# A planned order replaced by a written list, and key products in half-width tiles, in the first part of a delta-rule attention and two MoE layers

## The chip, the cores and the metric

One core of one Trainium2 chip runs the whole program in one launch. The metric is the device time in microseconds. The five engines are TensorE (PE; its weight loads are shown apart as PEld), VectorE (DVE), ScalarE (ACT), GpSimd (POOL) and SyncE (SP), which issues most of the DMA transfers.

## The reference

Three stages run one after the other. The first is a delta-rule attention over 4 batches, 8 heads, 768 steps and a head width of 48, which is written as a recurrence:

```python
k_n = k / (norm(k, axis=-1) + 1e-06)
for t in range(S):
    y[:, :, t] = einsum('bhd,bhde->bhe', q[:, :, t], state)
    v_old = einsum('bhde,bhd->bhe', state, k_n[:, :, t])
    state = state + beta[:, :, t] * einsum('bhd,bhe->bhde', k_n[:, :, t], v[:, :, t] - v_old)
```

Its output, as 3072 tokens of 384 numbers, goes through a dense layer `g = h * clip(h + 3, 0, 6) / 6` with `h = x @ w_in` (384 to 2048) and `g @ w_out`. The last stage sends every token to the one of 8 experts with the largest gate logit, `max(x @ w1, 0) @ w2` with a hidden width of 1024, and scales the result by the gate's probability.

## The kernel before

**The first part** (up to line 1156) computes the attention in chunks of 64 steps. One iteration `it` is one chunk of one pair of batches: 12 chunks by 2 pairs make 24 iterations, and four iterations make a group `g`, of which there are 6. In one iteration ScalarE and VectorE (in the first group; GpSimd later) split the normalised keys into two float16 halves `Kbd`, a transposing DMA turns them into `KG` or `KTb`, and TensorE forms the products of the keys with each other, `pG` (`g_stream`, line 603). Per head `u` these are two 64x64 blocks, one for each batch of the pair, on 64x64 tiles of the array, each in three products of halves. The blocks' two 32x32 diagonal blocks lie in columns 0 to 31 for the first 32 rows and in columns 32 to 63 for the others, so ScalarE copies them to `Dt` in four copies of 32 partitions each (lines 624 to 627). The columns 0 to 31, which hold the off-diagonal block, go to `MC`.

When a group's four iterations are copied, `t_stream` (line 634) transposes `Dt` on VectorE into `Bt`, multiplies it by beta on GpSimd (line 645) and clears `Xp` on ScalarE. Then `s_stream` (the solver, line 651) does 31 steps of two VectorE instructions each (`sub`, `Xp`), every step on what the step before has left. `z_stream` transposes the result, splits it into `TT` and multiplies it with `MC` (`pZ`). The two `chain` streams carry the state from chunk to chunk (`pR`, `pW`, `pS`), `o_stream` and `x_stream` make the attention's output `pO` and transpose it (`pX`, `xTH`, `xTL`), and `m_stream` (line 1029) runs the first 7 of the 16 hidden tiles of the dense layer for each chunk of 256 tokens: nine matmuls `ph`, four steps on ScalarE, VectorE, ScalarE and GpSimd (`t`, `t`, `gH`, `gL`), and six matmuls `py`. `wi_stream` and `wo_stream` prepare the weights of these tiles (`nws` on VectorE).

**The order** is not written by hand. Every stream is a generator that yields one instruction, or one burst of matmuls, at a time. `drive` (line 1078) asks a planner, `Clock`, when each stream's next instruction could start by its cost formulas, takes those that could start at about the same time on one engine, and emits the one with the smallest due number (`DUE`). `pin` ties each instruction to the one before on its engine, so that the queues of all engines and of SP run in the emitted order. In the planner's formulas a VectorE instruction that reads two SBUF operands waits for a running GpSimd instruction (`shared`, `unshared`), and not the other way round. `take` gives a stream one of three PSUM banks.

**The rest** is not touched by the change: the other 9 hidden tiles in six blocks of 512 tokens (line 1438 on, with the routing), and the experts (line 1548 on).

Of the kernel before, what the change touches and what calls it, by code (L numbers as in the profile page):

```python
# [24 lines left out]
class Op:  # L25

    tiles = 2
# [11 lines left out]
class Clock:  # L39


    def __init__(self, tc):
        self.tc, self.last = tc, {}
        self.free = dict(pe=0.0, act=0.0, dve=600.0, pool=3100.0, dma=0.0)
        self.columns = {}
        self.written, self.read, self.bus, self.issue = {}, {}, 0.0, 0.0
        self.slot, self.count, self.parts = {}, {}, {}
        self.runs, self.phase, self.tick, self.warm = [], 0.0, 0, False
        self.mode = 128, False
        self.place, self.end = {}, dict(act=0.0, dve=0.0)  # L50

    def tile(self, pool, shape, dt, tag, bufs, name):
        t = pool.tile(shape, dt, tag=tag, name=name, bufs=bufs)
        n = self.count[tag] = self.count.get(tag, -1) + 1
        self.slot[t.name] = (tag, n % bufs)
        return t

    def keys(self, ap):

        n = ap.name  # L60
        if n in self.parts:
            return [(n, x) for x in self.parts[n](ap)]
        return [self.slot.get(n, n)]

    def cost(self, op):

        n = 1
        for d in (op.ins[0] if "reduce" in op.fn.__name__ else op.out).shape[1:]:
            n *= d
        if "dma" in op.fn.__name__:  # L70
            return 40
        half = (op.ins[-1] if op.eng == "pe" else op.out).dtype in (FP16, FP32R, BF16)
        if op.eng == "pe":
            if op.ins[-1].dtype == FP32R:
                return n / 2.2
            if op.ins[-1].shape[0] <= 64:
                return max(32 if op.ins[-1].shape[0] == 64 else 25.2, n / 2.4) / op.tiles
            return max(25.5, n / 2.4 + 2.5) if half else 0.85 * max(n, 128)
        fn = op.fn.__name__
        pointers = sum(x.free_size() == 1 for x in op.ins[1:])  # L80
        if op.eng == "act":
            return (52 if op.ins[0].space == PSUM else 109) + 95 * (pointers > 0) + 84 * (len(op.outs) > 1) + 0.836 * n
        if op.eng == "dve":
            if half and fn == "tensor_copy":
                return 64 + 0.26 * n
            if fn == "memset":
                return 60 + (0.38 if half else 0.82) * n
            if fn == "transpose":
                return 70 + 1.06 * n
            if fn == "reciprocal":  # L90
                return 70 + 6 * n
            if fn == "tensor_scalar" and op.ins[0].space != PSUM:
                return 66 + 0.52 * n + 60 * (pointers > 0)
            return 70 + (0.52 if all(x.dtype == FP16 for x in op.ins) else 1.04) * n + 60 * (pointers > 0)
        if op.eng == "pool":
            if fn in ("memset", "tensor_copy"):
                return 80 + 0.81 * n
            wide = op.out.dtype == FP32R or op.out.shape[-1] == 32
            return 60 + (2.5 if wide else 2.15) * n
        raise ValueError(op.eng)  # L100

    def places(self, op):

        r, w = {}, (op.out.space, op.out.start_partition())
        for x in op.ins:
            r.setdefault(x.space, x.start_partition())
        return r, w

    def held(self, op):

        r, w = self.places(op)
        now = self.place.setdefault(op.eng, ({}, {}))
        return any(now[0].get(m, x) != x for m, x in r.items()) or now[1].get(w[0], w[1]) != w[1]

    def shared(self, op):

        if op.eng != "dve" or op.fn.__name__ in ("memset", "transpose", "tensor_reduce", "reciprocal"):
            return False
        wide = [x for x in op.ins if x.free_size() > 1]
        sb = [x for x in wide if x.space != PSUM]  # L120
        if op.fn.__name__ in ("tensor_copy", "tensor_scalar"):
            return bool(sb) and op.out.space != PSUM
        return len(sb) > 1

    def unshared(self, t):

        for a, b in reversed(self.runs):
            if b < t:
                break
            if a <= t:  # L130
                return b
        return t

    def matmul(self, op, t):

        n, tick = op.out.free_size(), int((t + self.phase) * 3 / 10240)
        rows = op.ins[-1].shape[0]
        half = op.ins[-1].dtype in (FP16, FP32R, BF16)
        while self.tick < tick:
            self.warm = self.columns.get(self.tick, 0.0) >= (3060 if self.warm else 3350)  # L140
            self.tick += 1
        self.columns[tick] = self.columns.get(tick, 0.0) + n * (1 if half else 2) * rows / 128
        mode, last = (32 if rows <= 32 else 64 if rows <= 64 else 128, op.ins[-1].dtype == FP32R), self.mode
        self.mode = mode
        turn = 90 * (mode[0] != last[0]) + (0 if mode[1] == last[1] else 85 if mode[1] else 13)
        if self.warm:
            return turn + self.cost(op)
        if rows <= 64:
            return turn + max(53.4 if rows == 64 else 42, n / 1.2) / op.tiles
        return turn + (max(27, n / 1.2) if half else 1.7 * max(n, 128))  # L150

    def ready(self, tiles):
        return max([self.free["pe"]] + [self.written.get(k, 0.0) for x in tiles for k in self.keys(x)])

    def start(self, ops):
        t = 0.0
        for op in ops:
            t = max([t] + [self.read.get(k, 0.0) for x in op.outs for k in self.keys(x)] + [self.written.get(k, 0.0) for x in op.ins for k in self.keys(x)])
        t = max(self.free[ops[0].eng], t + {"pe": 54, "pool": 77}.get(ops[0].eng, 33))
        if ops[0].eng in self.end and "dma" not in ops[0].fn.__name__ and self.held(ops[0]):  # L160
            t = max(t, self.end[ops[0].eng] + 13)
        return self.unshared(t) if self.shared(ops[0]) else t

    def pin(self, op):
# [5 lines left out]
        self.last[op.eng] = ins  # L170

    def emit(self, ops):
        t = t0 = self.start(ops)
        for op in ops:
            t += self.cost(op) if op.eng != "pe" else self.matmul(op, t)
            self.pin(op)
        self.free[ops[0].eng] = t
        if "dma" in ops[0].fn.__name__:
            o = ops[0].out
            n = 2 if o.dtype == FP16 else 4  # L180
            turn = "transpose" in ops[0].fn.__name__
            rate = 200 if turn else 170 if n * o.shape[-1] < 512 else 320
            for d in o.shape:
                n *= d
# [1445 lines left out]
```

## Time and profile before

| | us |
|---|---|
| median of three runs (lowest, highest) | 999.49 (997.93, 1002.62) |
| the profiled execution | 1003.64 |
| its span, first to last instruction | 1001.9 |
| first part, up to the first matmul of line 1459 | 507.6 |

| engine | busy us in the span | share |
|---|---|---|
| PE | 885.3 | 88% |
| DVE | 586.2 | 59% |
| ACT | 569.0 | 57% |
| POOL | 433.2 | 43% |

A share is a mean over stages with different limits, so it says little by itself. The first part has to be read in stretches, and the sections below do that. A row of the trace names the engine, the line (L36 is the helper that emits every instruction of the first part), the operation, and the tiles, output first.

### The profile page before, as it was taken

To read this page: it belongs to the slowest core of one execution; us is meant where nothing else is said; L and a number is where in the kernel's file an instruction comes from. 1 tells how busy PE (TensorE), PEld (TensorE's weight loads), DVE (VectorE), ACT (ScalarE), POOL (GpSimd) and SP (SyncE) were. 2 spreads that over 40 slices of the span, in tenths; PEclk is the share of its full clock that TensorE was granted. 3 is DMA by queue.
4 is the path that set the end of the run, shared out by engine and by line. 5 is a ranking of instruction groups with operands and counts; after the bars stand their busy time and mean duration, and the time that the engine had idled before them with its cause. 6 is when DMAs were issued, how large, how long until landed. Compare 5 with 4: busy or idle time off the path is not lost.

```text
span 1001.9 us, 27659 instructions
## 1 busy us (share of the span) xinstructions
PE 885.3 (88%) x11454; PEld 819.2 (82%) x11454; DVE 586.2 (59%) x1611; ACT 569.0 (57%) x1195; POOL 433.2 (43%) x446
## 2 busy tenths in 40 slices
PE   1423898889988899999989999999999999999997
PEld 1412888889888798888878899898899999999996
DVE  7888997888979789653487545554534211222221
ACT  4757889779888876755557333323334542455521
POOL 5255565455546524423343204223104936755761
PEclk9999799999999989999999999999999999999999
DMA  7978797996998956566365432332116734434500
GB/s 127 190 145 158 126 179 135 176 139 124 211 198 110 200 112 123 125 155 208 118 218 172 131 93 97 128 96 97 53 61 240 228 105 153 147 114 141 172 21 20
DMA packets 255080, 138.89 MB, mean 139 GB/s; under 512 B 199587, under 2 KB 239845, under 8 KB 254944
## 3 DMA queue, kind: packets, MB, share of 16 engines
q1 hardware_dynamic: 247120, 118.82, 53.5%
q0 software_dynamic: 7280, 17.41, 5.2%
q8 instruction: 91, 1.49, 0.6%
q10 hardware_dynamic: 544, 0.80, 0.2%
q14 instruction: 45, 0.37, 0.1%
HBM read 71.56 MB, written 35.50 MB: 107 GB/s over the span
## 4 chain that ended last, share of the span: by engine, by line
PE 61%; DVE 14%; ACT 8%; issue 7%; DMA 6%; POOL 4%; SPq 0%; POOLq 0%; ACTq 0%
PE ph L1459 11%; PE ph L1250 9%; PE py L36 5%; PE ph L36 5%; PE py L1475 3%; PE py L1474 3%; PE py L1473 3%; PE pz L1238 3%; PE pz L1240 3%; PE pz L1239 3%; DMA KG<-Kbd 2%; DVE Xp L36 2%; DVE sub L36 2%; PE pO L36 2%; PE pW L36 2%
## 5 line engine op out<-in xcount | busy, mean ns | idle before, releaser
L1254 DVE SCALAR_TENSOR_TENSOR hL<-ph,hH 128x384 fp32r<-128x384 f32 (+6 forms) x64 | 36.1, 564 | 163.6 <-ACT hH L1253 163.6
L36 POOL TENSOR_TENSOR gL<-t,gH 128x256 fp32r<-128x256 f32 x84 | 64.6, 769 | 130.8 <-ACT gH L36 122.6
L1253 ACT ACTIVATE hH<-ph 128x384 fp32r<-128x384 f32 (+6 forms) x64 | 31.6, 494 | 104.8 <-PE ph L1250 104.8
L1462 ACT ACTIVATE t<-ph,half 128x512 f32<-128x512 f32 x54 | 37.1, 687 | 76.4 <-PE ph L1459 75.2
L36 PE MATMUL ph<-xTH,wiH 128*128 128x256 f32 x252 | 76.4, 303 | 4.3 <-DVE t L36 3.4
L1419 POOL DMA_INDIRECT slots<-row,di x24 | 23.9, 997 | 125.1 <-DVE di L1411 119.7
L1463 DVE SCALAR_TENSOR_TENSOR t<-t,ph 128x512 f32<-128x512 f32 x54 | 37.1, 686 | 62.8 <-ACT t L1462 62.5
L1238 PE MATMUL pz<-a2H,hH 128*128 128x384 f32 (+1 forms) x216 | 73.2, 339 | 0.4 <-ACT hH L1253 0.4
L36 PE MATMUL ph<-xTL,wiH 128*128 128x256 f32 x252 | 72.2, 286 | 0.7 <-DVE xTL L36 0.7
L1240 PE MATMUL pz<-a2H,hL 128*128 128x384 f32 (+1 forms) x216 | 72.4, 335 | 0.0
L1239 PE MATMUL pz<-a2L,hH 128*128 128x384 f32 (+1 forms) x216 | 72.4, 335 | 0.0
L36 PE MATMUL ph<-xTH,wiL 128*128 128x256 f32 x252 | 71.6, 284 | 0.0
L1271 POOL DMA_INDIRECT out_dram<-yo,rw x29 | 28.0, 967 | 100.7 <-ACT yo L1270 96.5
L1467 DVE TENSOR_TENSOR gL<-t,gH 128x512 fp32r<-128x512 f32 x54 | 47.5, 882 | 32.6 <-ACT gH L1466 32.5
L36 DVE TENSOR_TENSOR Xp<-Xp,sub 128x31 f32<-128x31 f32 (+15 forms) x186 | 64.0, 344 | 2.8
L36 PE MATMUL py<-woH,gH 128*128 128x392 f32 x168 | 64.9, 386 | 0.7 <-issue 0.7
L36 DVE TENSOR_TENSOR sub<-Bt,Xp 128x31 f32<-128x31 f32 (+15 forms) x186 | 61.6, 331 | 2.2
L298 POOL TENSOR_TENSOR a2L<-r,a2H 128x384 fp32r<-128x384 f32 x64 | 62.5, 1009 | 0.0
L36 ACT ACTIVATE t<-ph,half 128x256 f32<-128x256 f32 x84 | 39.6, 471 | 38.4 <-PE ph L36 31.4
L298 POOL TENSOR_TENSOR a1L<-r,a1H 128x512 fp32r<-128x512 f32 x48 | 60.4, 1305 | 0.1
L36 PE MATMUL py<-woH,gL 128*128 128x392 f32 x168 | 58.7, 350 | 0.7 <-POOL gL L36 0.6
L36 DVE SCALAR_TENSOR_TENSOR t<-t,ph 128x256 f32<-128x256 f32 x84 | 35.0, 417 | 40.3 <-ACT t L36 39.3
(318 smaller groups left out, 3141.9 us busy)
## 6 DMA issues: line engine op xcount, KB each, us to landing
r<-in_moe_w_dram SPq DMA_DIRECT2D x32, 768.0 KB, 4.6
slots<-zrow SPq DMA_DIRECT2D x8, 784.0 KB, 6.2
stage<-in_moe_w_in_dram SPq DMA_DIRECT2D x16, 384.0 KB, 3.9
stage<-in_moe_w_out_dram SPq DMA_DIRECT2D x16, 384.0 KB, 3.2
row<-ypart SPq DMA_DIRECT2D x6, 784.0 KB, 4.5
ysave<-row SPq DMA_DIRECT2D x6, 784.0 KB, 3.9
rw<-slots SPq DMA_DIRECT2D x24, 196.0 KB, 3.1
kr<-in_k_dram SPq DMA_DIRECT2D x24, 192.0 KB, 4.6
```

The source lines that it names most:

```text
L36: return self.fn(*self.a, **self.k)
L298: in_order(pool.tensor_tensor(dst[1], src_ap, dst[0].bitcast(FP32), ALU.subtract))
L1238: pe.matmul(o, hh[:, ts_], a2[0][:, fp], start=fp == 0, stop=False)
L1239: pe.matmul(o, hh[:, ts_], a2[1][:, fp], start=False, stop=False)
L1240: pe.matmul(o, hl[:, ts_], a2[0][:, fp], start=False, stop=fp == KF2 - 1)
L1250: pe.matmul(ph, a1[a][:, c, fs], xt[x][:, c, 0:n], start=k == 0, stop=k == 3 * KD - 1)
L1253: act.activation(hH, ph, ACTF.Relu)
L1254: dve.scalar_tensor_tensor(hL, ph, 0.0, hH.bitcast(FP32), ALU.max, ALU.subtract)
L1459: pe.matmul(ph, wi(a, f)[:, c], xt[x][:, c], start=n == 0, stop=n == 3 * KD - 1)
L1462: act.activation(t_, ph, ACTF.Relu, bias=half, scale=1.0 / 6.0)
L1463: dve.scalar_tensor_tensor(t_, t_, 1.0, ph, ALU.min, ALU.mult)
L1467: dve.tensor_tensor(gL, t_, gH.bitcast(FP32), ALU.subtract)
```

## The change

The planner with its cost formulas and due numbers is taken out. `drive` now reads a list, `ORDER`, of 2926 characters. The k-th character of `ALPHABET` stands for the k-th stream, and each entry emits that stream's next instruction or burst. Entries that only wait for a stream's condition are passed when the condition holds, as before. A program outside the kernel made the list; the change's description says that it was searched with VectorE and GpSimd waiting for each other in both directions.

In `g_stream` each 64x64 block is formed by two tiles of 64 rows by 32 columns. For the first 32 rows the moving operand is the first 32 key columns, given twice, so that the diagonal block also stands in columns 32 to 63. Then one ScalarE copy of 128 partitions takes all diagonal blocks. In the first group the multiplication of `Bt` by beta moves from GpSimd to VectorE, and the squares of the keys alternate between two buffers (the second is `vsq`, which is there already).

```diff
-        clk = Clock(tc)
+        clk = Order(tc)
...
-                    sq_ = tmp([128, H, D], FP32, "ksq", 1)
+                    sq_ = tmp([128, H, D], FP32, "ksq" if g or j % 2 else "vsq")
...
-                yield [o for u in range(H) for o in halves(lambda r: (p_[r, u], [kt[r, x, u, r] for x in range(2)], [kt[r, x, u, r] for x in range(2)]), True, True)]
+                ops = []
+                for u in range(H):
+                    for n, (a, b) in enumerate(((0, 0), (0, 1), (1, 0))):
+                        for blk in range(2):
+                            for bb in range(2):
+                                k = slice(64 * bb, 64 * bb + 64)
+                                r = slice(64 * bb + 32 * blk, 64 * bb + 32 * blk + 32)
+                                x = kt[k, b, u, k] if blk else kt[k, b, u, r].unsqueeze(1).to_broadcast([64, 2, 32])
+                                o = p_[r, u] if blk else p_[r, u].rearrange("p (x t) -> p x t", x=2)
+                                ops.append(PE.matmul(o, kt[k, a, u, r], x, start=n == 0, stop=n == 2))
+                                ops[-1].tiles = 4
+                yield ops
...
-                for x in range(4):
-                    r = slice(32 * x, 32 * x + 32)
-                    c = slice(32 * (x % 2), 32 * (x % 2) + 32)
-                    yield ACT.activation(Dt[r, :, 8 * j:8 * j + 8], p_[r, :, c].rearrange("p u i -> p i u"), ACTF.Copy)
+                yield ACT.activation(Dt[:, :, 8 * j:8 * j + 8], p_[:, :, 32:64].rearrange("p u i -> p i u"), ACTF.Copy)
...
-                yield POOL.tensor_tensor(Bt, Bt, bY[:, g].unsqueeze(1).to_broadcast([128, 32, 32]), ALU.mult)
+                yield (POOL if g else DVE).tensor_tensor(Bt, Bt, bY[:, g].unsqueeze(1).to_broadcast([128, 32, 32]), ALU.mult)
...
+            for n in [ALPHABET.index(c) for c in "".join(ORDER)]:
+                if isinstance(now[n], tuple):
+                    assert now[n][0] == "take" and now[n][1]() is not None, (n, now[n])
+                    step(n)
+                assert isinstance(now[n], list), (n, now[n])
+                clk.emit(now[n])
+                step(n)
+                settle()
...
+        ALPHABET = "0123456789abcdefghijklmnopqrstu"
+        ORDER = [
+            "kkksrskrksssrraasrsjsrbbbsaasbsrpkrsbpbbsbsbbbbbbbqrqbnnqqnnqqsnqoonrsqnqqnpnqpsqnqnsor0ondjjdnsnqnq",
...
```

## Rows read from the trace of the kernel before

**Rows 1.** Busy time of each engine by stretch: the span's start, us, then the engines.
```profile
0.00:51.00 51.00, 14.83 (x227) 12.69 (x227) 38.96 (x118) 29.60 (x71) 22.12 (x28) 1.00 0.93 159
51.00:124.00 73.00, 33.84 (x875) 31.12 (x876) 64.49 (x197) 51.41 (x104) 39.43 (x38) 0.92 0.77 141
124.00:400.00 276.00, 251.82 (x5926) 236.15 (x5925) 237.84 (x723) 226.87 (x493) 134.84 (x132) 0.98 0.89 156
400.00:484.00 84.00, 79.62 (x1598) 73.48 (x1596) 42.51 (x101) 52.98 (x115) 28.95 (x32) 1.00 0.53 146
484.00:508.00 24.00, 21.26 (x124) 18.24 (x125) 13.05 (x38) 11.81 (x28) 9.37 (x12) 0.93 0.48 152
508.00:1001.90 493.90, 483.96 (x2710) 447.48 (x2708) 189.37 (x440) 196.37 (x389) 198.46 (x206) 0.99 0.39 125
```

**Rows 2.** VectorE's waits from 0 to 400 us: total, times, longest.
```profile
DVE t L36 <- ACT t L36: 8.8, 8, 2.2
DVE W L36 <- ACT W L36: 6.1, 7, 1.9
DVE uL L36 <- ACT uH L36: 5.3, 4, 2.2
DVE ss L36 <- ACT ksq L36: 4.0, 7, 0.8
DVE MC L36 <- ACT MC L36: 3.8, 4, 2.2
```

**Rows 3.** Tile pG, all its instructions: duration min/median/max in ns, first and last start.
```profile
L36 PE MATMUL pG<-KG x960: 186/193/259, 67.4 to 350.7; 64*64 64x64 f16 x192
L36 ACT ACTIVATE Dt<-pG x96: 356/374/378, 36.0 to 352.1; 32x256 f32<-32x256 f32 x96
L36 ACT ACTIVATE MC<-pG x24: 373/383/384, 38.6 to 352.5; 128x256 f16<-128x256 f32 x24
```

**Rows 4.** Timeline, ScalarE and VectorE: first and last of 18 waits behind Dt copies.
```profile
37.30 0.66 DVE L36 TENSOR_TENSOR Kbd<-kn,Kbd 64x384 f16<-64x384 f32 x1 [0.61 <-ACT Kbd L36]
...
346.86 0.76 ACT L36 ACTIVATE Dt<-pG 32x256 f32<-32x256 f32 x2
347.65 0.63 ACT L36 ACTIVATE Pst<-pm 128x512 f16<-128x512 f32 x1
348.30 0.38 ACT L36 ACTIVATE MC<-pG 128x256 f16<-128x256 f32 x1
...
348.72 0.42 DVE L36 SCALAR_TENSOR_TENSOR MC<-pG,MC 128x256 f16<-128x256 f32 x1 [2.23 <-ACT MC L36]
```

**Rows 5.** Timeline of the start, up to the solver's first step.
```profile
1.84 4.09 SPq L36 DMA_DIRECT2D kr<-in_k_dram  x4
...
9.44 0.55 DVE L36 TENSOR_REDUCE ss<-ksq 128x8 f32<-128x384 f32 x1 [0.57 <-ACT ksq L36]
...
51.19 2.35 POOL L36 TENSOR_TENSOR Bt<-Bt,bY 128x1024 f32<-128x1024 f32 x1
...
51.96 0.55 DVE L36 TENSOR_REDUCE ss<-ksq 128x8 f32<-128x384 f32 x1 [0.49 <-ACT ksq L36]
...
53.10 0.55 DVE L36 TENSOR_REDUCE ss<-ksq 128x8 f32<-128x384 f32 x1 [0.59 <-ACT ksq L36]
53.57 0.18 DVE L36 TENSOR_TENSOR sub<-Bt,Xp 128x31 f32<-128x31 f32 x1
```

**Rows 6.** Timeline of TensorE: one burst each of pG and pZ.
```profile
158.43 0.94 PE L36 MATMUL pG<-KG 64*64 64x64 f16 x48
...
407.14 0.76 PE L36 MATMUL pZ<-TT,MC 32*32 32x32 f16 x48
```

**Rows 7.** Tiles Xp and TT on VectorE, duration and first and last start.
```profile
L36 DVE STREAM_TRANSPOSE Bt<-Xp x6: 1241/1246/1250, 87.1 to 399.3; 128x1024 f32<-128x1024 f32 x6
L36 DVE COPY W<-TT x48: 239/276/1015, 97.3 to 432.6; 32x512 f16<-32x512 f16 x48
```

**Rows 8.** A VectorE group up to 508 us: busy, mean ns of one, idle before.
```profile
L36 DVE TENSOR_TENSOR Xp<-Xp,sub 128x255 f32<-128x255 f32 x12 | 5.1, 425 | 0.2
```

**Rows 9.** The chain that ended last: start, us, what.
```profile
478.57 1.63 PE pO L36 x96
```

More of the change, by code (lines that the diff above doesn't have):

```diff
@@ L36, in now @@
         return self.fn(*self.a, **self.k)
-class Clock:
+class Order:
     def __init__(self, tc):
         self.tc, self.last = tc, {}
[L44 to L50, printed above, removed]
-    def tile(self, pool, shape, dt, tag, bufs, name):
[L53 to L162, printed above, removed]
@@ L164, in pin @@
+    def tile(self, pool, shape, dt, tag, bufs, name):
+        return pool.tile(shape, dt, tag=tag, name=name, bufs=bufs)
     def pin(self, op):
@@ L1078, in drive, with step @@
         def drive(streams):
-            st = []
-            for n, (gen, due) in enumerate(zip(streams, DUE)):
-                due = [float(x) for x in due.split()]
-                st.append([None, due, n, gen, due.pop(0)])
-            def step(x):
+            now = [None] * len(streams)
+            def step(n):
+                now[n] = "next"
+                while now[n] == "next":
+                    now[n] = next(streams[n], None)
+                if now[n] is not None and not isinstance(now[n], (tuple, list)):
+                    now[n] = [now[n]]
@@ L1086, in step, with settle @@
+            def settle():
                 while True:
[L1087 to L1089 removed]
+                    go = [n for n, x in enumerate(now) if isinstance(x, tuple) and x[0] == "need" and x[1]()]
+                    if not go:
                         return
[L1091 to L1095 removed]
@@ L1097, in start @@
-            def start(x):
-                y = x[0]
-                if isinstance(y, tuple):
-                    ok = y[1]()
-                    return ok if y[0] == "take" and ok is not None else -1.0 if ok else None
-                return clk.start(y)
-            for x in list(st):
-                step(x)
-            while st:
-                ready = [(start(x), x[2], x) for x in st]
-                ready = [x for x in ready if x[0] is not None]
-                assert ready, [x[3].__name__ for x in st]
-                t, _, x = min(ready, key=lambda y: y[:2])
-                if isinstance(x[0], list):
-                    eng = x[0][0].eng
-                    end = t + TOL * sum(clk.cost(o) for o in x[0])
-                    same = [y for y in ready if isinstance(y[2][0], list) and y[2][0][0].eng == eng and y[0] <= end]
-                    t, _, x = min(same, key=lambda y: (y[2][4], y[0]))
-                    clk.emit(x[0])
-                step(x)
```

83 lines of the change are left out of this document (36 added, 47 removed), and 31 rows, old and new, of the table DUE.

## The prediction

> **What bounds the kernel now.** I read the page's slices first: TensorE is dense from an eighth of the span on, VectorE until four tenths. Then I cut the span into stretches [rows 1]. To 51 us, before the solver's first step, VectorE is busy 38.96 us of 51 and TensorE 14.83. From 51 to 124 us, until the dense layer begins, VectorE is busy 64.49 of 73. From 124 to 400 us three engines are tight together: TensorE 251.82 of 276 (91%), VectorE 237.84 (86%), ScalarE 226.87 (82%). From 400 to 508 us TensorE alone is (100.88 of 108), and after 508 us, which the change leaves alone, it is busy 483.96 of 493.9. The place to look at is VectorE before 400 us. The sixth solver's result is transposed at 399.3 us [rows 7], and the multiplication that needs it starts on TensorE at 407.14 us [rows 6]. Behind it lie 100 us of TensorE work with some 7 us of idle time, so the first part can end earlier only if that point comes earlier. VectorE's idle time up to 400 us is 400 - 38.96 - 64.49 - 237.84 = 58.7 us, and its largest causes are waits for ScalarE: five kinds alone make 28.0 us [rows 2]. So ScalarE, 18% idle itself, costs time because its queue is in order: a short product of VectorE's stands behind a ScalarE copy that stands behind others.
>
> **Is the new order another schedule?** The list can be read: each letter is the next entry of one stream, and the streams' entries stand in the code. I counted what the list puts ahead of a point in VectorE's queue, and what the trace has there. Ahead of the first solver's diagonal (the copy into Xp) the list has 91 entries, the trace 115; ahead of the first solver's closing transpose 205 against 223; ahead of the sixth's 1029 against 1032. On TensorE the sixth group's multiplication comes after the second hidden tile of the ninth chunk, in the trace after the first. So the schedule is the old one in outline: the same work precedes the point that counts and the same follows it. The entries moved away at the start come back later, and nothing is gained by them as such. Any gain is VectorE's idle time before 400 us, filled.
>
> **Part by part.**
>
> *One diagonal copy.* Four copies at 374 ns become one of 128x256, whose nearest row is the copy into MC at 383 ns [rows 3]: 4 x 374 - 383 = 1.11 us of ScalarE per iteration, 26.7 us over 24. That is work off an engine that isn't the bound, so I count only the VectorE waits that it stands behind. I followed each wait of VectorE on ScalarE back through ScalarE's unbroken run of work: 18 of those waits stand behind Dt copies, from 37.30 us to 348.72 us [rows 4]. In the last, VectorE sits 2.23 us for MC while ScalarE works through four Dt copies and others; three copies fewer take 1.1 us off. Taking three quarters of the Dt time in each run, and never more than the wait, the 18 give 11.3 us: 3.0 before 124 us, 8.3 after. This is the most it can give by waits as they stand; the least is nothing, if what VectorE needs next is late too. I take 8.3 times VectorE's busy share of 0.86, which is 7 us, and leave the early 3.0 to the next term.
>
> *The start.* The second buffer for squares removes waits such as the 0.57 us at 9.44 us [rows 5]. The list sets the first output weights' conversion ahead of the first squares, into time in which VectorE sat idle, 51 - 38.96 = 12.0 us in this stretch [rows 1]. Against it stand the queues it passes: its load goes ahead of the first key load on SP, whose four issues take 4.09 us [rows 5], so about 1 us each; and the squares queue behind its steps on ScalarE. From -7 (more than half of the idle time) to +1.5 (a late key load with nothing filled); I take -2.5.
>
> *Beta on VectorE in group 0.* GpSimd's multiplication takes 2.35 us, and the first step follows at 53.57 us; in between VectorE worked and sat idle 0.49 + 0.59 = 1.1 us [rows 5]. On VectorE the price, from 0.18 us for 31 elements [rows 5] and 0.425 for 255 [rows 8], is 1.1 ns an element, so 1.3 us for 1024. It swaps 1.1 us of idle time for 1.3 of work: 0, within 1.3 either way.
>
> *The products in 64x32 tiles.* A burst grows from 48 to 96 matmuls of 64 columns. Now 48 take 0.94 us, the last one's own 0.19 included [rows 6, 3], so (0.94 - 0.19)/47 = 16 ns each with two tiles in turn. The trace has no four tiles in turn. If the time belongs to a tile, 32 ns, four share it, 8 ns each, and the burst costs what it does now. The shortest spacing in the trace is that of pZ, on 32x32 tiles: 0.76 us, by the same sum 12 ns. At that pace 96 take 95 x 12 + 190 = 1.33 us, 0.39 more; at the old 16 ns 0.77 more. The 20 bursts after 67 us (960 rows by 48 [rows 3]) would bring 0 to 8, or 15 us, on an engine that is 91% busy. I take 10 ns, 0.2 us a burst, 4 us of work, and half of it on the path: +2. [...]
>
> *The rest of the order.* The search's other rule, GpSimd waiting for VectorE as well, aims at instructions stretched by the other engine: a copy of W takes 276 ns in the median and 1015 at worst [rows 7]. All such stretches above 40 ns in the first part, measured against each form's lower quartile, make 14 us on VectorE in 30 instructions. Together with the 30 us of idle time from 124 to 400 us (276 - 237.84 = 38.2, less 8.3), some of which a better order fills, this goes from -17 to +12, the latter if the list trusts durations that the chip doesn't have. The nearest rows say that most of it is no matter of order, since the work ahead is equal; I take -1.5.
>
> *Sum:* -7 - 2.5 + 0 + 2 - 1.5 = -9. The profiled execution took 1003.64 us for a span of 1001.9, so it becomes 994.6; it lay 4.15 above the median of the runs, 999.49, and against that the forecast is 990.5.
>
> **Rivals.**
>
> *The tiles don't run four at a time* (slower). Its place is pG from 67 to 351 us; its price at 16 ns is 20 x 0.77 = 15 us, all on the path if TensorE's other work stands behind it. It decides from 0.55 us more a burst on, a spacing of 14 ns, where its 11 us cancel the other terms (7 + 2.5 + 1.5). With 15 in place of the +2: -11 + 15 = +4, so 1003.5. For it: both rows of bursts use only two tiles in turn. Against it: 96 matmuls of 48 columns on 64x64 tiles take 1.63 us [rows 9], (1.63 - 0.19)/95 = 15 ns each, hardly less than those of 64 columns, so the pace belongs to a tile and not to its columns. 18%.
>
> *Hidden anyway.* TensorE idles only 24 us from 124 to 400 us [rows 1]; if it, not VectorE, sets the pace there, ScalarE's 27 us buy nothing but more idle time: within 2 us of 999.5. For it: TensorE's 91% against VectorE's 86%. Against it: TensorE's busy time holds matmuls that only drain. 20%.
>
> *The order does much more.* If half of VectorE's 38.2 idle us from 124 to 400 us go (19, the 7 included) and 7 at the start: -26, so 973.5. For it: idle time is there, and TensorE's dense layer begins with VectorE. Against it: equal work ahead of each point. 20%.
>
> **How the numbers follow.** Forecast 42%, its own range 984 to 997. The range takes in the hidden case and half of each outer one: 973 to 1004. A difference of 0.5%, 5 us, is about what can be told from no change: faster than 994.5 is 0.40 of the forecast's 0.42 and the order's 0.20, 0.60; within, 0.02 and 0.20, 0.22; slower, 0.18.
>
> **What would show it.** Dt: 24 copies near 0.38 us, and ScalarE 27 us less busy. The burst of 96 matmuls: 0.95 us right, 1.4 or more for the first rival. VectorE's idle time before the sixth closing transpose near 48 us instead of 59, and that transpose near 390 us. The distance from it to the first matmul of line 1459, now 108 us, unchanged. The forecast is wrong if the transpose comes earlier and that distance grows by as much, or if VectorE's waits on ScalarE stay at their sum.

## The result, and the profile after

The changed kernel takes 1011.93 us (median of 13 executions) against 1001.95 for the kernel before in the same measurement: a ratio of 1.0087, 95% interval 1.0067 to 1.0107. In a later measurement on another chip the same kernel took 1006.29 (1.0058, interval 1.0036 to 1.0080). It is slower, by 10.0 and 5.0 us; the forecast was 990.5, 9 us faster than the kernel before, and the range ended at 1004. Since one kernel's median moves by 5.6 us from one measurement to another, kernels are compared below within one measurement wherever that is possible, and by their ratios otherwise.

The page of the changed kernel: span, engines, the granted clock in 40 slices (tenths of full speed), and the queue of instruction packets (100 of 16 KB, 91 before: 9 more for 2304 more matmuls and loads, one for 256 of them; the 25212 here are 98.5 times 256, the 22908 before 89.5 times, so they are TensorE's). TensorE has 12606 matmuls and as many weight loads, 1152 of each more than before (24 bursts of 48), and ScalarE is busy 540.9 us, 28 less.

```profile
span 1010.8 us, 29883 instructions
...
PE 894.3 (88%) x12606; PEld 828.8 (82%) x12606; DVE 591.7 (59%) x1612; ACT 540.9 (54%) x1123; POOL 430.6 (43%) x445
...
PEclk9999798989888999999999999999999999999999
...
q8 instruction: 100, 1.64, 0.7%
```

Busy time by stretch, cut at the same events where they moved [rows 1]: stretch, its length, then PE, PEld, DVE, ACT, POOL with instruction counts, then granted clock, DMA share, GB/s.

```profile
0.00:51.00 51.00, 14.28 (x417) 12.22 (x417) 44.83 (x100) 23.66 (x55) 21.43 (x27) 1.00 0.89 153
51.00:124.00 73.00, 38.33 (x1180) 34.84 (x1181) 69.67 (x226) 48.73 (x98) 36.85 (x37) 0.95 0.90 160
124.00:411.60 287.60, 259.92 (x6592) 244.04 (x6592) 232.64 (x708) 206.65 (x440) 134.43 (x132) 0.92 0.78 144
411.60:495.00 83.40, 79.15 (x1596) 74.41 (x1591) 44.41 (x106) 52.49 (x113) 30.08 (x32) 0.98 0.63 169
...
518.50:1010.80 492.30, 482.15 (x2710) 446.31 (x2708) 186.28 (x435) 196.38 (x388) 197.77 (x198) 1.00 0.39 124
```

The start is better, as forecast: VectorE is busy 44.83 us of the first 51, before 38.96. The third row has the loss: the stretch is 11.6 us longer, and the granted clock is 0.92 instead of 0.98. In windows of 1 us the granted clock reads 1.00 or 0.50, but for 13 of 1001 windows before and 21 of 1010 here that lie where it changes from one to the other; so a mean below 1.00 is read as time at half. Added up over these windows, 43 us of this stretch are at half, against 12 us before. After it the stretches are 0.6, 0.5 and 1.6 us shorter than before. (Line 1459 of the kernel before is line 1304 in the changed one; the text keeps the first number.)

The tiles that the change touches [rows 3], and the solver's closing transpose [rows 7]. The last columns of a row are min/median/max in ns and the first and last start. There are 24 diagonal copies at 374 ns, and the first closing transpose comes 3.3 us earlier, but the sixth at 410.9 us, 11.6 later than before.

```profile
L36 PE MATMUL pG<-KG x1920: 186/194/239, 63.6 to 360.3; 64*32 64x64 f16 x192
...
L36 ACT ACTIVATE Dt<-pG x24: 356/374/393, 32.7 to 361.2; 128x256 f32<-128x256 f32 x24
```

```profile
L36 DVE STREAM_TRANSPOSE Bt<-Xp x6: 1237/1249/1250, 83.8 to 410.9; 128x1024 f32<-128x1024 f32 x6
```

TensorE's timeline around four bursts, the answer to [rows 6]: start, us, what, and in brackets how long TensorE sat idle before it and for what. "issue" means that it waited for nothing that the profile shows.

```profile
134.52 0.95 PE L36 MATMUL pG<-KG 64*32 64x64 f16 x96
...
152.28 0.92 PE L36 MATMUL pG<-KG 64*32 64x64 f16 x92
155.11 0.21 PE L36 MATMUL pG<-KG 64*32 64x64 f16 x4 [1.91 <-issue]
...
257.11 0.52 PE L36 MATMUL pG<-KG 64*32 64x64 f16 x45
260.24 0.88 PE L36 MATMUL pG<-KG 64*32 64x64 f16 x51 [2.61 <-issue]
...
297.16 1.04 PE L36 MATMUL pG<-KG 64*32 64x64 f16 x96
301.21 0.20 PE L36 MATMUL pO<-uH,Pst 64*64 64x48 f16 x1 [2.52 <-issue]
```

The first burst is the one that was hoped for: 96 matmuls in 0.95 us, four tiles in turn. The other three show the loss: TensorE stops in the middle of a burst or right behind it, for 1.9 to 2.6 us, with no wait that the profile shows. After 55 us there are 22 of these stops, 24.9 us in all, and each of them lies at a packet of the instruction queue; before there were 5, 4.9 us. The largest groups in the list of TensorE's waits (total, times, longest), changed kernel and then before:

```profile
PE pZ L36 <- issue: 7.1, 4, 3.3
PE pO L36 <- issue: 6.5, 4, 2.5
PE pG L36 <- issue: 5.7, 5, 2.6
```

```profile
PE pW L36 <- issue: 1.8, 1, 1.8
```

From the packet's start to TensorE's next matmul it is 2.2 to 2.9 us in the stops of 0.8 us or more. And the stops keep step with the packets: counted in TensorE's matmuls from the start, they come after 986, 1497, 1880, 2135, 2262, 2646 and so on, and from each of the 22 to the next it is a multiple of 128 matmuls (with their loads 256 instructions), less two at most.

To compare kernels I use one sum, TensorE's first part up to the first matmul of line 1459: idle time before a matmul or weight load that has no wait of its own in the trace ("stops"), what of it lies at instruction packets, idle time that waits for VectorE, the rest of the idle time, and the time in which it runs. The stops that lie at no packet, 9 to 14 us in every row, are nearly all ahead of 55 us, and the list of waits puts them down to VectorE or a DMA (in the changed kernel one of 12.0 us, pwt for nws). They are no loss of the kind meant here and nearly the same in all kernels of the list; so differences of the stops hold to 1 or 2 us within the list, while from before to the changed kernel it is 20.0 us at packets, and not 36.8 - 13.8 = 23.0.

```
us, one profiled execution each    1459 starts at  stops  at packets  VectorE  other  runs
before                                507.6        13.8     4.9       44.5     33.7   401.5
changed                               518.1        36.8    24.9       31.7     28.6   412.1
changed, second measurement           510.1        39.4    27.5       29.4     27.2   405.2
list, 64x64 tiles (e1)                503.1        22.9    11.7       40.3     29.9   401.0
list, 64x64 tiles, paired (e12)       502.2        23.1    11.9       39.0     29.9   401.3
old order, 64x32 tiles (e5)           517.0        22.3    13.2       45.8     32.9   401.4
list, 64x64 cut in two (e6)           524.8        28.5    17.3       32.2     25.9   429.3
list, 64x32, one product (e7)         487.2        21.5     9.3       40.9     31.1   384.8
list, 64x64, one product (e8)         501.0        22.0     8.3       52.4     31.7   386.0
list, 64x32, two products (e13)       496.2        25.8    14.6       32.9     30.4   398.2
```

(The first matmul, where the count begins, is at 14.1 us before, 14.5 in e5 and 8.9 in all others.)

### The profile page after: what moved, and what is told of

The parts are those of the page before. It is cut to its first block, busy times and chain, and to the rows that moved or that the text cites. A ratio compares the mean times of both kernels' runs of the same rounds, so it can differ in the third digit from the quotient of the medians.

```text
span 1010.8 us, 29883 instructions
## 1 busy us (share of the span) xinstructions
PE 894.3 (88%) x12606; PEld 828.8 (82%) x12606; DVE 591.7 (59%) x1612; ACT 540.9 (54%) x1123; POOL 430.6 (43%) x445
## 4 chain that ended last, share of the span: by engine, by line
PE 72%; DVE 13%; issue 7%; POOL 3%; ACT 3%; DMA 2%; SPq 0%; POOLq 0%; ACTq 0%
PE ph L1304 11%; PE ph L1095 9%; PE ph L36 8%; PE py L36 8%; PE pO L36 4%; PE py L1320 3%; PE py L1318 3%; PE py L1319 3%; PE pz L1083 3%; PE pz L1085 3%; PE pz L1084 3%; PE pW L36 3%; DVE nw L36 2%; PE pG L36 2%; DVE Xp L36 2%
## 5 line engine op out<-in xcount | busy, mean ns | idle before, releaser
L36 PE MATMUL ph<-xTH,wiH 128*128 128x256 f32 x252 | 76.7, 305 | 11.6 <-DVE t L36 11.2
L36 PEld LDWEIGHTS ph<-xTH,wiH 128*128 128x128 f32 x252 | 48.4, 192 | 19.7 <-DVE t L36 18.6
L36 ACT ACTIVATE t<-ph,half 128x256 f32<-128x256 f32 x84 | 39.6, 472 | 45.8 <-PE ph L36 40.7
L36 PE MATMUL py<-woH,gL 128*128 128x392 f32 x168 | 60.8, 362 | 0.3 <-POOL gL L36 0.3
```

The lines of the kernel that those rows point to most:

```text
L36: return self.fn(*self.a, **self.k)
```

## Experiments

The first four separate the two halves of the change, the list and the tiles.

**e1: the list with the old tiles.** The products and the diagonal copies of the kernel before, in the order of the list:

```
-  ops.append(PE.matmul(o, kt[k, a, u, r], x, ...))             # 96 of 64x32
+  yield [o for u in range(H) for o in halves(...)]             # 48 of 64x64
-  yield ACT.activation(Dt[:, :, 8 * j:8 * j + 8], p_[:, :, 32:64]...)
+  yield [ACT.activation(Dt[32 * x:32 * x + 32, ...]) for x in range(4)]
```

> The list's order is kept; the key products go back to 64x64 tiles (48 matmuls a burst) and the diagonal blocks to four copies, emitted where the one copy stood. Theory A (TensorE runs out of instructions: 96 matmuls with 96 weight loads in 0.75 us use them up faster than they are fetched): TensorE's idle time with no releaser in the first part falls from 36.8 us to 14 to 20, the half-clock stretches shrink, and the time is 994 to 1003 us. Theory B (the list fits the chip badly): the waits stay, ScalarE's 27 us come back, 1012 to 1020 us.

Measured: 997.44 us, ratio 0.9966 (0.9951 to 0.9982). The list alone makes the kernel faster; the loss comes with the tiles. The time is in theory A's range and out of B's. Stops are 22.9 us, some 14 less than with 64x32 tiles, but more than the 14 to 20 that A expected: at packets they are 11.7 us, against 4.9 before with as many instructions. So the order counts beside the number, and the list gains although it has more stops.

**e2: the tiles without the list.** The kernel before with the 64x32 products and the one copy; its planner, which prices instructions, then makes its own order.

> The kernel before with its planner, and only the 64x32 tiles and the single diagonal copy of the change. Theory A: idle time of TensorE with no releaser rises from 13.8 us to 25 to 40 in the first part, with breaks inside bursts of pG and just behind them; 1004 to 1014 us. Theory B: the tiles as such cost nothing and ScalarE is 27 us freer: 988 to 1000 us.

Measured: 1046.36 us, ratio 1.0448 (1.0421 to 1.0474), far worse than any theory said. The stretches of its trace, columns as above:

```profile
51.00:124.00 73.00, 32.58 (x1078) 29.84 (x1079) 64.54 (x197) 43.16 (x85) 39.39 (x38) 0.55 0.76 141
124.00:400.00 276.00, 236.39 (x5954) 220.32 (x5942) 207.60 (x616) 193.09 (x407) 122.79 (x120) 0.90 0.79 140
400.00:554.50 154.50, 140.46 (x2461) 127.74 (x2461) 89.28 (x244) 88.81 (x186) 49.20 (x56) 0.96 0.54 132
```

The granted clock is 0.55 before the dense layer and 0.90 and 0.96 behind, and the first part ends at 554.5 us, 47 later than before; 14 of them are stops and 23 are TensorE running longer. Two things are mixed here, the tiles and a new order; e5 separates them.

**e3: the new tiles for the first eight of 24 steps only,** 64x64 and four copies for the rest (`if it < 8:` around the two forms above).

> The list's order; 64x32 tiles and one copy in the iterations 0 to 7 only, where TensorE has little to do; 64x64 tiles and four copies in the other 16. Theory A: as with 64x64 tiles throughout, or better at the start: 992 to 1001 us. Theory B: 1010 to 1018 us.

Measured: 997.52 us, ratio 0.9962 (0.9941 to 0.9984), the same as e1. Those eight bursts are over by 95 us, ahead of TensorE's dense stretch, and there the new tiles cost nothing and bring nothing.

**e4: bursts split in two,** the second half of 48 matmuls held back until the next products of the dense layer are out, or until an instruction that needs it must go. In the trace 10 of the 16 bursts after 120 us come apart, by 1 to 5 us, and 6 stay whole.

```
+  if n == 22 and len(now[n]) == 96:
+      held.append(now[n][48:])
+      now[n] = now[n][:48]
```

> The changed kernel, but each burst of 96 key products is cut in two, and the second half is put behind the next dense-layer matmuls on TensorE where the entries in between allow it. Same number of instructions, thinner in time. Theory A: part of the breaks go, 1003 to 1010 us. Theory B: only more changes between kinds of matmul, 1012 to 1017 us.

Measured: 1013.41 us, ratio 1.0124 (1.0099 to 1.0149), with stops of 35.1 us: no better than whole bursts, so theory A's range was missed, and the time is in theory B's. Thinning ten bursts by a few microseconds did not help; by e10's pace of supply, the added instructions of a burst alone need 1.4 us.

**e5: the old order with the new tiles.** The kernel before plans with its old products and copies, and what is issued in their place are the new ones:

```
+  planned = [o for u in range(H) for o in halves(...)]
+  for n, o in enumerate(planned):
+      o.real = ops[2 * n:2 * n + 2]
+  yield planned
```

> The planner's order of the kernel before, entry for entry and with its beta on GpSimd, but each burst of 48 products of 64x64 is issued as 96 of 64x32, and the one full diagonal copy stands where the first of the four stood. Theory S (the number of TensorE instructions is what costs: 192 in a microsecond with their weight loads, and TensorE waits for its instruction stream in the middle of a burst, after which the granted clock falls): slower than before by what the tiles cost in the list's order, about 14 us less what the copies save, 1004 to 1018 us, TensorE's idle time without a releaser ahead of the second part 25 to 40 us instead of 13.8, half-clock time 40 us or more instead of 27. Theory P (the tiles cost little in themselves, and the 1046 us of the replanned kernel came of the order that the planner made from them): 993 to 1004 us. If the tile's form alone lowers the clock in every order: 1030 us or more, half-clock time over 100 us.

Measured: 1013.81 us, ratio 1.0111 (1.0069 to 1.0153), inside theory S's range; theory P is out. The excess of e2 over this was its new order. This is the cleanest view of the cost: against the kernel before TensorE runs 401.4 us against 401.5, its waits for VectorE are 45.8 us against 44.5, the clock is no worse (about 24 us at half against 27), and the first part is 9.4 us longer, 8.5 of which are stops (8.3 at packets). VectorE is held up with it: its waits for TensorE ahead of the sixth transpose add up to 17.4 us, before 9.9. S was wrong on the clock, of which it expected 40 us or more at half, and its 25 to 40 us of stops were 22.3. One of the stops, on e5's timeline:

```profile
338.75 0.34 PE L36 MATMUL py<-woL,gH 128*128 128x392 f32 x1
338.93 0.34 PE L36 MATMUL py<-woH,gL 128*128 128x392 f32 x1
339.20 0.95 PE L36 MATMUL pG<-KG 64*32 64x64 f16 x96
340.08 0.21 PE L36 MATMUL pO<-Spr01H,QTb 64*64 64x48 f16 x2
340.13 0.19 PE L36 MATMUL pO<-Spr01L,QTb 64*64 64x48 f16 x2
340.16 0.19 PE L36 MATMUL pO<-Spr01H,QTb 64*64 64x48 f16 x1
342.74 0.20 PE L36 MATMUL pO<-Spr01H,QTb 64*64 64x48 f16 x1 [2.39 <-issue]
```

The burst runs at full pace, and five matmuls into the next one TensorE stops for 2.39 us, with no wait that the profile shows.

**e6: as many instructions, other tiles.** 64x64 weights, each product in two matmuls of 32 columns, so 96 a burst again, and the four copies.

```
+  for c in range(2):
+      for n, (a, b) in enumerate(((0, 0), (0, 1), (1, 0))):
+          for bb in range(2):
+              ops.append(PE.matmul(p_[k, u, c_], kt[k, a, u, k], kt[k, b, u, ...]))
```

> The changed kernel with the old 64x64 weights and the four copies, but each product cut into two of 32 columns: 96 TensorE matmuls a burst as in the 64x32 form, with the 64x64 form's two tiles at a time. Theory S (number of instructions): as slow as the changed kernel or slower, 1006 to 1020 us, idle time without a releaser 30 us or more, half-clock time 40 us or more. Theory F (the 64x32 form: four tiles of 64x32 do not hold the clock as two of 64x64 do): like the list with whole 64x64 tiles, 996 to 1004 us, idle time without a releaser about 23 us, half-clock time about 20 us; up to 24 bursts times 0.6 us more if a matmul of 32 columns takes as long as one of 64.

Measured: 1020.48 us, ratio 1.0187 (1.0150 to 1.0225). A burst takes 1.69 us:

```profile
185.54 1.69 PE L36 MATMUL pG<-KG 64*64 64x32 f16 x96
```

Against e1, in a different measurement, the first part is 21.7 us longer: 28.3 more of running time, of which 22.9 are the longer bursts (pG is busy 50.1 us against 27.2), and 5.6 us more of stops, less 8.1 us of waits for VectorE and 4.0 of others. So a doubled count brings stops to 64x64 tiles too, though S was off on all three sizes: 28.5 us is under its 30, the half-clock time of 37.5 us under its 40, and the time half a microsecond over its 1020. The time does not decide against theory F: matmuls of 32 columns did take as long as those of 64, for which F allowed up to 14 us more, and the longer bursts account for most of the excess. Against F stand the stops and the half clock, which it expected near 23 and 20 us.

**e7 and e8: one product of three.** The changed kernel, and the list with 64x64 tiles and four copies, both without the two products that hold a low half: 32 and 16 matmuls a burst.

```
-  for n, (a, b) in enumerate(((0, 0), (0, 1), (1, 0))):
+  for n, (a, b) in enumerate(((0, 0),)):
```

> The changed kernel with only the first of the three products of a pair of halves (32 matmuls of 64x32 a burst instead of 96; the two products with the low half are left out). Theory S: fewer instructions than the list with 64x64 tiles had (48), so at or under its 997 us: 985 to 998 us, idle time without a releaser 23 us or less, half-clock time 25 us or less. Theory F: the form still costs, 1003 to 1014 us, half-clock time 40 us or more.

> The list with 64x64 tiles, four copies and only the first of the three products (16 matmuls a burst; the two products with the low half are left out): beside the 64x32 kernel with one product it leaves the form alone as the difference. Theory S: 983 to 997 us, within 4 us of that one, and 16 instructions a burst less bring little; idle time without a releaser 23 us or less. Theory F: 983 to 997 us, and 10 us or more faster than that one.

Measured: 982.52 us, ratio 0.9801 (0.9765 to 0.9837), for 64x32, and 995.79, ratio 0.9938 (0.9912 to 0.9964), for 64x64. With few instructions the 64x32 form is faster by 13.3 us, the other way round than theory F said, and more than the 4 us that S allowed; e7 is also 2.5 us under S's range. F is out by this pair. TensorE runs as long in both (384.8 and 386.0 us), and what differs beside the tiles is the copy. Here is the closing transpose in e7 and then in e8:

```profile
L36 DVE STREAM_TRANSPOSE Bt<-Xp x6: 1236/1249/1250, 82.8 to 382.4; 128x1024 f32<-128x1024 f32 x6
```

```profile
L36 DVE STREAM_TRANSPOSE Bt<-Xp x6: 1240/1249/1250, 83.9 to 395.9; 128x1024 f32<-128x1024 f32 x6
```

The sixth comes 13.5 us earlier with one copy. VectorE's idle time ahead of it is 38.2 us against 51.7, and its waits for ScalarE, added up, are 18.4 us against 35.4. That is the term that the prediction put at 7 us, and it seems to be worth more once TensorE can use it; the copy was not changed by itself. In e8, which saves 15 us of TensorE's running time against e1, that saving turns into waits for VectorE (52.4 us against 40.3).

**e9: fewer instructions for the same products.** First a control: in each tile the two products with the same weights stand one behind the other. Then the second of each pair was marked to need no weight load.

```
+  for few in (((0, 0), (0, 1)), ((1, 0),)):
+      for blk in range(2):
+          for bb in range(2): ...
+  ins = e.add_instruction(mybir.InstMatmult(..., ldweights=False, ...))   # second kernel only
```

> The changed kernel with the products of a 64x32 burst in another order only: in each tile the two products with the high half as weights stand one behind the other. Still 96 matmuls and 96 weight loads a burst. A control for the next kernel. Every theory: like the changed kernel, 1008 to 1016 us, unless two matmuls running in one tile in turn hold up the other three tiles; then the burst is longer than 0.95 us, by up to 0.25 us, and the time up to 6 us more.

> The control with one thing less: the second product of each pair is issued as a matmul without a weight load of its own, since the tile still holds the same weights. 96 matmuls and 64 weight loads a burst, 160 instructions instead of 192, the same matrix products. Theory S (TensorE waits for its instruction stream): instruction packets ahead of the second part 74 instead of 77, TensorE's idle time at their fetches some 18 to 21 us instead of 24.9 (the list with 64x64 tiles, 96 instructions a burst, had 11.7), and 3 to 7 us faster than the control. Rival (the loads lie beside the matmuls and cost nothing; the loss of the tiles is elsewhere): within 2 us of the control.

Measured: 1004.95 us (ratio 1.0050, 1.0027 to 1.0074) and 1004.94 (1.0046, 1.0023 to 1.0069). The control is under its range of 1008 to 1016 us, which e12 to e14 explain. The mark had no effect: the second trace also has 12606 weight loads and 100 instruction packets. So the pair decides nothing about S; it only tells that two kernels with as many instructions of each kind agree.

**e11: the same mark in all bursts of small tiles,** and their products paired.

> The changed kernel with weights kept in every burst of small tiles: the key products (64 loads instead of 96 a burst), the output products of 64x64 (64 instead of 96) and the products of 32x32 behind the solver (32 instead of 48): some 80 instructions less for each of 24 steps, 7 packets of 256. Theory S: 70 packets ahead of the second part, about what the list with 64x64 tiles has (68), so idle time at fetches 11 to 16 us instead of 24.9, with the one copy's gain kept: 993 to 1003 us, faster than the kernel before or the same. Rival: 1008 us or more.

Measured: 1004.94 us (1.0051, 1.0023 to 1.0079), again with 12606 loads and 100 packets. Inconclusive for the same reason.

**e10: a long run of nothing but small matmuls.** In the seventh burst the work is done eight times in 64x64 tiles and eight times in 64x32 tiles, ahead of the burst itself.

```
+  if it == 6:
+      ops = sum([wide() for _ in range(8)], []) + sum([again() for _ in range(8)], []) + ops
```

> The changed kernel, and in the seventh burst of key products the work is repeated: eight times in 64x64 tiles (384 matmuls), then eight times in 64x32 tiles (768 matmuls), then the burst as before, one behind another with nothing to wait for. What TensorE does when its instructions come one after another. Theory S: the 64x64 part runs near its pace in a short burst, 0.95 to 1.3 us per 48, that is 96 instructions; the 64x32 part runs at 0.95 us per 96 only for the first two or three hundred matmuls, and then with stops of 1 to 2 us at each instruction packet, on average 1.6 to 2.2 us per 96 matmuls (192 instructions). Rival (no limit of supply): 0.95 us per 96 throughout, and no stops. The whole kernel's time is no measure here: 15 to 30 us more.

Measured, on TensorE's timeline:

```profile
85.46 4.01 PE L36 MATMUL pG<-KG 64*64 64x64 f16 x205
90.43 2.21 PE L36 MATMUL pG<-KG 64*64 64x64 f16 x128 [0.96 <-issue]
93.88 1.70 PE L36 MATMUL pG<-KG 64*64 64x64 f16 x128 [1.24 <-issue]
97.88 1.21 PE L36 MATMUL pG<-KG 64*32 64x64 f16 x128 [2.30 <-issue]
101.61 1.89 PE L36 MATMUL pG<-KG 64*32 64x64 f16 x128 [2.52 <-issue]
105.34 1.89 PE L36 MATMUL pG<-KG 64*32 64x64 f16 x128 [1.83 <-issue]
108.80 1.89 PE L36 MATMUL pG<-KG 64*32 64x64 f16 x128 [1.56 <-issue]
112.52 1.90 PE L36 MATMUL pG<-KG 64*32 64x64 f16 x128 [1.83 <-issue]
116.25 1.89 PE L36 MATMUL pG<-KG 64*32 64x64 f16 x128 [1.83 <-issue]
119.98 0.45 PE L36 MATMUL pG<-KG 64*32 64x64 f16 x19 [1.83 <-issue]
```

and the DMA traffic from 90 to 120 us, of which there is nothing but this (packets, MB, share):

```profile
q8 instruction: 8, 0.13, 1.9%
```

128 matmuls with their 128 weight loads, then a stop, and so on. Eight packets of 0.13 MB together are 16 KB each; at 256 instructions to a packet that is 64 bytes an instruction, by my estimate. From 97.88 to 119.98 us there are six rounds, 3.68 us each: 14.4 ns an instruction. The one round that is all 64x64, from 90.43 to 93.88 us, takes 3.45 us; the next, to 97.88 us, has 51 matmuls of 64x64 and 77 of 64x32 (a row merges them) and takes 4.00. The mean of the two is 3.7 us as well. The pace belongs, within that scatter, to neither tile, and not to the clock either, which the stretches show (columns as above):

```profile
90.00:95.00 5.00, 3.33 (x207) 3.18 (x210) 0.00 (x0) 0.00 (x0) 1.38 (x2) 1.00 0.03 7
95.00:100.00 5.00, 1.80 (x202) 1.58 (x186) 0.00 (x0) 0.00 (x0) 0.00 (x0) 1.00 0.01 3
100.00:105.00 5.00, 1.89 (x128) 1.75 (x128) 0.00 (x0) 0.00 (x0) 0.00 (x0) 0.56 0.02 3
105.00:110.00 5.00, 3.10 (x221) 2.95 (x224) 0.00 (x0) 0.00 (x0) 0.00 (x0) 0.50 0.01 3
```

At the full clock 128 matmuls of 64x32 take 1.21 us and at half 1.89, and the next packet ends the round after the same 3.7. Two of theory S's sizes were off: the 64x64 part is held up as well, and 96 matmuls (192 instructions) take 2.8 us on average, not 1.6 to 2.2. "No limit of supply" is out. The clock fell, to 0.56 in the mean from 100 to 105 us, behind a stretch in which TensorE was busy 1.80 us of 5, and it read 0.50 from 105 to 125 us, past the last of these stops, which ended at 119.98 us.

The trace has one packet of 16 KB for 128 loads and 128 matmuls, and the first stop of the run comes after 205 matmuls, 410 instructions with their loads. How many instructions TensorE holds ahead, no run here measures.

**e12, e13, e14, in one measurement:** the list with 64x64 tiles and all bursts paired as in e9, the changed kernel with two of the three products (without the one that has the low half as weights), and the changed kernel once more.

> The list with 64x64 tiles and four copies (997.4 us), and in each burst of small tiles (key products, output products, products behind the solver) the two products with the same weights stand one behind the other, as in the paired control. If that order gives 7 us wherever it is used: 988 to 993 us. If it helped the changed kernel only by the way its stops and clock falls came to lie: 995 to 1000 us.

> The changed kernel with two of the three products (64 matmuls and 128 instructions a burst; the product with the low half as weights is left out): between the one with one product (982.5 us, idle at fetches 9.3 us, half-clock time 24) and the changed kernel (1011.9, 24.9 and 55). TensorE's work alone would put it 7 us above the first: 988 to 992 us, if stops and clock falls stay as there. Theory S: idle at fetches 12 to 20 us and the time 993 to 1003 us.

> The changed kernel once more, for a second profiled execution. If the stops belong to the instruction stream, they come at the same instructions: idle at fetches 23 to 27 us. If its half-clock time (54.6 us in the first profile) belongs to the order of its products and not to one execution, 45 us or more again; if it varies from execution to execution, 25 to 45 us. Time 1008 to 1015 us.

Measured: 998.78 us (ratio 0.9974, 0.9954 to 0.9995), 992.00 (0.9917, 0.9899 to 0.9936) and 1006.29 (1.0058, 1.0036 to 1.0080). Pairing brings nothing, and the 7 us that e9's control seemed to gain over the changed kernel were the distance between two measurements: by ratio the control's 1.0050 and e14's 1.0058 agree. e14 itself is 2 us under its range of 1008 to 1015. In its profiled execution there are again 22 stops at instruction packets, 27.5 us, where the first had 24.9, and 19 of them come after the same number of matmuls as in the first; its half-clock time is 37.5 us beyond 100 us, where the first had 54.6, and 13.7 us more lie ahead of 100 us, where the first had none. So the stops belong to the program, and where the clock is at half varies.

The stretch of the dense layer in e12 and then in e14 (columns as above):

```profile
124.00:397.10 273.10, 247.50 (x5809) 233.12 (x5806) 230.68 (x706) 222.20 (x484) 134.62 (x132) 0.97 0.79 150
```

```profile
124.00:403.10 279.10, 248.24 (x6420) 232.70 (x6419) 227.59 (x692) 202.00 (x430) 130.16 (x130) 0.94 0.77 146
```

From e12 to e14 line 1459 starts 7.9 us later: stops +16.3, TensorE's running time +3.9 (more of it at half clock), waits for VectorE -9.6, other waits -2.7. And by the number of products in a burst, at one form and one copy: 32 matmuls 982.5 us with 9.3 us of stops at packets, 64 matmuls 992.0 with 14.6, 96 matmuls 1006.3 with 27.5 (the first from another measurement). From 64 to 96 the first part grows by 13.9 us, 13.6 of which are stops and 7.0 running time, less 3.5 and 3.2 of other waits. Theory S's range for e13 began 1 us above what it took, and its 992.0 us is the upper end of what TensorE's work alone gave (988 to 992, with stops as at one product); the stops at packets, 14.6 us against 9.3, are in S's range of 12 to 20.

## Why the prediction was wrong

**The step that failed** is "The products in 64x32 tiles", put at +2. Its pace held: 96 matmuls take 0.95 us, 8 ns each, where it took 10. So its first rival fell: the four half-width tiles, two on each half of the rows, took a matmul every 8 ns, the two whole ones every 16 [rows 6]. But the step priced the burst by its length alone and put the supply of instructions at nothing. Each matmul here comes with a weight load (12606 of each), and 96 of them are 192 instructions in 0.95 us, 4.9 ns each, where e10 measured a supply of 14.4 ns each. Even the old burst, 96 instructions in 0.94 us where that supply would need 1.4, must by these numbers live on instructions fetched ahead. The new one needs 192 x 14.4 = 2.8 us of supply and the burst of pO next to it, [rows 9], as much for its 1.63 us; during dense matmuls the stock can recover, by my estimate (two of 392 columns start 0.18 us apart in e5's rows, 90 ns an instruction). That the stops grow by 8.5 us in the old order (e5) and 16.3 in the list (e12 to e14), and not by 24 x 1.4 us, the added supply, I put down to this recovery; it was not tested by itself. In place of +2 the tiles, with the one copy's saving in it, made the first part 9.4 us longer in the old order (before to e5) and 7.9 us in the list (e12 to e14). In the trace of before the stops were there, five at packets with 4.9 us, as "issue", and the prediction never asked what they were.

**One diagonal copy, -7:** the work saved was right (ScalarE is 28.1 us less busy, 27 expected), its effect on the path was not. With TensorE relieved, e8 to e7 is 13.3 us, though there the tiles change too. In the changed kernel the gain does not arrive: VectorE's idle time ahead of the sixth transpose is 64.5 us, not 48, and its waits for ScalarE are 40.7 us, before 36.2 (61.5 and 36.2 us in the second execution): they did not fall, which the prediction had named as a sign of being wrong. The largest of them:

```profile
DVE t L36 <- ACT t L36: 13.0, 14, 2.5
DVE W L36 <- ACT W L36: 8.9, 6, 3.0
DVE uL L36 <- ACT uH L36: 6.2, 9, 1.8
```

The wait for t, the dense layer's activation, grew from 8.8 us [rows 2]. ScalarE takes t from TensorE's products, so an engine that TensorE's stops hold up holds up VectorE. This is read from the waits, e5's 17.4 us among them, and no run changes it alone. The prediction had VectorE as the pace and TensorE as a follower before 400 us, and there they pace each other. The rival "hidden anyway" had this mechanism, with a gain of nothing where there was a loss.

**The start, -2.5, and the rest of the order, -1.5:** the sum came out, the place is not shown. e1, which is these two terms and beta, gained 3.4 us on the kernel before in the same measurement, where -4 was forecast. But in e1's profile the sixth transpose is only 1.1 us earlier (398.2 us against 399.3), and 3.3 us lie behind it, where the prediction expected nothing; so the agreement is in part luck. The reading that the list is the old schedule in outline stands.

**The 100 us behind the sixth transpose** nearly stayed: 107.2 us from it to line 1459 (518.1 - 410.9), before 108.3; in the second execution it is 104.9, as in e1. The place of the loss, ahead of the transpose, was right, the sign of what happens there wrong.

**The range** had 15 us for the tiles as an upper end, about what they cost in stops in the list (16.3 us from e12 to e14), but for a reason that didn't hold, and only with the rival's chance of 18%. That the price was near was luck. Some 2.5 us of the miss is no change at all: the kernel before took 1001.95 us beside the changed one, and 999.49 where the forecast started.

Left open: e4 did not show that stops can be thinned away, and why a packet starts only when TensorE has run dry at some places (at 257.60 us for the stop from 257.63), but earlier at others (at 166.17 for the stop from 167.38), was not found. That the half clock follows the stops is seen in e10 (0.50 from 105 us on) and fits the changed kernel (TensorE stops from 257.63 to 260.24 us, and the clock is at half from 259.4 to 266.3); in e5 there were 8.5 us more of stops and no more half clock, so which stops bring it stays open. No version with the full products and one copy beat the list with 64x64 tiles: e1 and e3, at 0.9966 and 0.9962, are the fastest that compute everything.

## What to carry to other kernels

Count instructions as well as time: here each matmul came with a weight load, two instructions, and in e10 a run of small tiles went on at 14.4 ns an instruction after the first 410, though a burst in 64x32 tiles runs at 8 ns a matmul (96 in 0.95 us). A smaller tile that doubles the count can save work on other engines and still lose where TensorE is dense, as here: ScalarE was 28 us less busy, and the stops at packets went from 4.9 us to 24.9; look for idle time without a releaser, and hold it against the instruction queue's packets. And test the halves of a change alone: here the list gained 0.3%, and with the tiles the kernel was 0.6 to 0.9% slower.

## What the runs showed of the hardware

TensorE's instructions came in packets of 16 KB, one for 256 of them (9 packets more for 2304 instructions more), and a stop of 0.8 us or more at one lasted until 2.2 to 2.9 us after the packet's start, though the packet itself took 1.0 us (median of the changed kernel's 100). Back to back, 256 instructions took 3.7 us on average, at the granted clock 1.00 and at 0.50 (e10). At the full clock four 64x32 tiles in turn ran at 8 ns a matmul (96 in 0.95 us), and two 64x64 tiles with matmuls of 32 columns at (1.69 - 0.18) / 95 = 16 ns (e6), the same as with 64 columns [rows 6]: the pace of a tile did not depend on its columns here.
